# Retention attention with a routed expert layer, on one core: the tail's products ahead of the evictions in each half unit

## The chip, the core and the metric

The kernel runs on one core of a Trainium2 chip. The engines work side by side, each through its own row of instructions in a fixed order: TensorE (PE, and PEld for its weight loads) multiplies matrices into PSUM, VectorE (DVE) and ScalarE (ACT) read PSUM and work elementwise, GpSimd (POOL) does elementwise work and issues transfers, SyncE (SP) issues transfers. An instruction starts when the one before it on its engine lets it and the semaphores that it waits for have their values. The metric is the time of one execution on the device, in microseconds; less is better. TensorE's granted clock stands in the profile as a share of 2.4 GHz; 0.50 is 1.2 GHz.

## The reference

Two layers. The first is attention without a softmax: the scores of each head are weighted by a power of a per-head factor and by causality. The second sends each of 4608 tokens to one of 8 experts, 576 each.

```python
scores = scale * np.matmul(q, k.transpose(0, 1, 3, 2))        # q, k, v: 8 x 8 heads x 576 x 64
gamma = 1.0 - 2.0 ** (-5.0 - np.arange(H, dtype=np.float32))
rel = pos[:, None] - pos[None, :]
Dmat = np.where(rel >= 0, gamma[:, None, None] ** rel[None, :, :], 0.0)
attn = np.matmul(scores * Dmat[None, :, :, :], v)

logits = x @ w_gate                                           # x: 4608 x 512, the attention's output
# tokens are given to experts in order of their logits, 576 to each
for e in range(E):
    h = np.maximum(x[mask] @ w1[e], 0.0)
    out[mask] = h @ w2[e]
```

## The kernel before

**Three stages.** The attention runs until about 158 us; then the tokens are routed (logits, counting, a search for the threshold of each expert); from about 190 us on the experts' two matrix products fill TensorE to the end. All that the change touches is in the attention.

**A unit.** The attention has 16 units, `u` = 0 to 15; one unit is two heads of each of two batch entries. The 576 tokens of a head are four chunks of 128 and a tail of 64. The weighting by powers is split: the values are scaled by one power as they come in (`vscale`, on GpSimd), and the results are multiplied by another as they leave PSUM (`evict`). What remains is a causal mask inside a chunk and, across chunks, a running sum of k times v, the state.

**A half unit.** Each unit has two passes through the loop at line 769, `hf` = 0 for chunks 0 and 1, `hf` = 1 for chunks 2 and 3 and the tail. In a pass stand, in this order:

- `A` (L564): the scores of the next half unit, 8 products into the tile `pA`, and VectorE's mask (L566) on them into `am`. There is one buffer of `pA`, so the next scores wait until the mask has read the last ones. With `hf` = 0 also `A2`, the tail's scores (L575) and their mask (L577).
- `across` (L599): the products of queries with the state, into `pX`, the tile that collects the results; one buffer, two PSUM banks of 512 columns, of which 256 are for chunks 2 and 3 and 64 for the tail.
- `ST` (L587): one chunk's products of keys and values added to the state in `pS`, and ScalarE's copy of it (L589).
- `within` (L608): masked scores times values, into `pX`.
- `evict` (L628): VectorE multiplies the results by their powers on the way from `pX` to `xT`.
- `ST` once more, for the next chunk (with `hf` = 1 that is chunk 0 of the next unit).
- With `hf` = 1: the tail's products, `within2` (L615) and `across` for chunk 4 (L599), and the tail's `evict` (L628, 128x128).
- `fills`: the routing's work, put by hand at numbered places `g` (nine in a unit): logits (`logits`, L641 and L647; `logits2`, L654 and L656), transposes of rows (L665), the counting's tables.

In the last unit the second eviction is cut in two, chunk 2 and chunk 3.

**What sets the order.** The instructions of every engine stand in the order in which this code calls them (`tc.manual_schedule()`); no scheduler moves them. A layer beneath puts in the waits: an instruction that touches a tile waits for the earlier ones that wrote or read the same stretch of it. It takes a strided access as one stretch from its first to its last column, so the tail's columns of `pX` count as touched by the eviction of chunks 2 and 3, and the other way round.

**Loads.** `ahead` calls the loads of unit `u + 2` during unit `u`, with three buffers each; they stand on SyncE in one row with the stores of finished rows to DRAM (L670), which wait for VectorE's transposes (L665).

Of the kernel before, what the change touches and what calls it, by code (L numbers as in the profile page):

```python
# [497 lines left out]
def attention(tc, nc, P, qk, vk, cst_d, wg_d, rf, xd, Lg):  # L498
# [69 lines left out]
    def A2(u):  # L568

        k, q = LD[u, 'k'], LD[u, 'q']  # L570
        pa = P['ps'].tile([128, 2, 64], F32, name="pAt", tag="y", bufs=2)
        for h in range(2):
            for r in range(2):
                s = slice(1024 + 64*(h ^ r), 1088 + 64*(h ^ r))
                nc.tensor.matmul(pa[half(r), h], k[half(r), s], q[half(r), s], start=True, stop=True, skip_group_check=True)  # L575
        AM[u, 2] = P['w'].tile([128, 2, 64], F32, name="amt", bufs=2)
        nc.vector.tensor_tensor(AM[u, 2], pa, m2[:, None, :].to_broadcast([128, 2, 64]), op=ALU.mult)  # L577

    def ST(u, c):

        if u == 16: return
        if c == 0: PS[u] = PS2[:, 2*(u % 2):2*(u % 2)+2]
        v, n = LD[u, 'v'], LD[u, 'n']
        for b in range(2):
            for h in range(2):
                s = slice(256*c + 128*b + 64*h, 256*c + 128*b + 64*h + 64)
                nc.tensor.matmul(PS[u][half(h ^ b), b], n[:, s], v[:, s], start=(c == 0 and b == 0), stop=False, skip_group_check=True)  # L587
        st = P['w'].tile([128, 2, 64], F32, name="S", bufs=4)
        nc.scalar.activation(st, PS[u], AF.Copy)  # L589
        SI[u, c] = st  # L590

    def across(u, cs):

        q = LD[u, 'q']
        for c in cs:
            for h, b in FOUR:
                r = half(h ^ b)
                o, a = (PX[u, c//2][half(h), b, 128*(c % 2):128*(c % 2)+128], 256*c + 128*b) if c < 4 else (PX[u, 1][half(h), b, 256:320], 1024 + 64*b)
                nc.tensor.matmul(o, SI[u, c-1][r, b, :], q[r, a:a+o.shape[1]], start=c in (1, 2), stop=False, skip_group_check=True)  # L599

    def within(u, hf):

        v = LD[u, 'v']
        for j in range(4):
            c, b = divmod(j, 2)
            for h in range(2):
                a = 512*hf + 128*j + 64*h
                nc.tensor.matmul(PX[u, hf][half(h), b, 128*c:128*c+128], v[:, a:a+64], AM[u, hf][:, h ^ b, j],  # L608
                                 start=False, stop=False, skip_group_check=True)
# [8 lines left out]
    def evict(u, c0, c1):  # L618

        bp, hp = divmod(u, HP)  # L620
        if c0 == 4:
            src, dst, e = PX[u, 1][:, :, 256:320], XT[bp][:, hp, 1024:].rearrange("p (b i) -> p b i", b=2), ex[:, hp, None, 512:].to_broadcast([128, 2, 64])
        else:
            n, o = c1 - c0, 128*(c0 % 2)
            src = PX[u, c0//2][:, :, o:o+128*n].rearrange("p b (c i) -> p b c i", i=128)
            dst = XT[bp][:, hp, 256*c0:256*c1].rearrange("p (c b i) -> p b c i", b=2, i=128)
            e = ex[:, hp, None, 128*c0:128*c1].rearrange("p o (c i) -> p o c i", i=128).to_broadcast([128, 2, n, 128])
        nc.vector.tensor_tensor(dst, src, e, op=ALU.mult)  # L628
# [83 lines left out]
    for bp in range(NP):  # L712
        g0 = (bp+1)*4*NB + 2
        for k, b0 in enumerate((0, 3, 6)):
# [3 lines left out]
            c0 = bp*NB + b0  # L718
# [30 lines left out]
    def ahead(g):  # L749

        u, blk = divmod(g, NB)
        if u + 2 < 16:
            if blk == 3:
                load(u + 2, "kq")
            if blk == 5:
                load(u + 2, "v")
            if blk == 6:
                load(u + 2, "n")
        if u + 1 < 16:
            if blk == 2:  # L760
                vscale(u + 1, 0, 4)
            if blk == 5:
                vscale(u + 1, 4, 9)

    def fills(gs):
        for g in gs:
            for f, a in fill.get(g, []): f(*a)

    for u in range(16):
        for hf in range(2):  # L770
            gs = range(NB*u + 4*hf, NB*u + 4 + 5*hf)
            for g in gs:
                ahead(g)
            if hf == 0 and u % HP == 0:
                XT[u//HP] = P['xt'].tile([128, HP, 1152], F32, name="xT")
            A(u + hf, 1 - hf)
            if hf == 0:
                A2(u)
            PX[u, hf] = two.tile([128, 2, 512], F32, name="pX", tag="X", bufs=1)
            across(u, (2, 3) if hf else (1,))  # L780
            ST(u, 1 + 2*hf)
            within(u, hf)
            if u == 15 and hf:
                for c in (2, 3):
                    evict(u, c, c + 1)
            else:
                evict(u, 2*hf, 2*hf + 2)
            ST(u + hf, 2 - 2*hf)
            if hf:
                within2(u)  # L790
                across(u, (4,))
                evict(u, 4, 5)
            fills(gs)
    P['close']()
# [16 lines left out]
    c = R.first_digits(30, 36)  # L811
# [320 lines left out]
```

## Time and profile before

| | |
|---|---|
| median of 3 runs | 666.03 us (663.08 to 666.48) |
| the profiled execution: device time | 664.57 us |
| the profiled execution: span | 662.8 us |
| TensorE busy | 613.2 us, 93% of the span |
| VectorE busy | 418.0 us, 63% |
| ScalarE busy | 244.8 us, 37% |
| GpSimd busy | 179.0 us, 27% |
| chain that ended last, share by engine | TensorE 66%, VectorE 17%, DMA 8% |

The span runs from the first to the last instruction in the trace; the device time has the start and end around it. The shares are averages over the three stages, and in the experts' stage TensorE alone is full; so what the change is worth is read from the timeline before 165 us, unit by unit: a row of it gives when an engine starts a group of equal instructions, for how long, and, in brackets, how long the engine had been idle and what ended that. Matmuls overlap, so the spacing of two starts says more than their lengths.

### The profile page before, as it was taken

How to read it: one execution, taken by the hardware profiler on the slowest of the kernel's cores; microseconds unless marked ns; L12 is line 12 of the kernel's file. 1: busy time of each engine (PE TensorE's matmuls, PEld its weight loads, DVE VectorE, ACT ScalarE, POOL GpSimd, SP SyncE). 2: the span in 40 equal slices, each digit the busy share in tenths (PEclk: the TensorE clock that was granted, in tenths of full speed). 3: DMA queues.
4: the chain of work that ended last, by engine and by line, in shares of the span. 5: the costliest groups of instructions: out<-in, count | busy, mean ns of one | idle time of the engine just before them, and what ended most of it. 6: DMA issues, size and time to landing. Idle time of an engine off the chain costs nothing.

```text
span 662.8 us, 14684 instructions
## 1 busy us (share of the span) xinstructions
PE 613.2 (93%) x5756; PEld 522.0 (79%) x5756; DVE 418.0 (63%) x1504; ACT 244.8 (37%) x424; POOL 179.0 (27%) x221
## 2 busy tenths in 40 slices
PE   7889797978887998999999999999999999999995
PEld 5777676756557886987897798879879989988974
DVE  3586968778864987888897799689775302311200
ACT  1111020112235434455356146424624734653501
POOL 2331122120041107125143241323224135131111
PEclk8999897998997999999999999999999999999998
DMA  9996797973459548969589749928975896893521
GB/s 328 401 372 205 251 332 257 300 242 95 145 176 231 112 142 223 234 182 235 173 197 243 205 116 214 254 83 204 233 203 139 203 255 165 191 248 110 97 63 40
DMA packets 51702, 134.19 MB, mean 202 GB/s; under 512 B 5810, under 2 KB 19762, under 8 KB 51634
## 3 DMA queue, kind: packets, MB, share of 16 engines
q1 hardware_dynamic: 36530, 81.08, 35.8%
q0 software_dynamic: 14960, 51.91, 35.4%
q8 instruction: 45, 0.74, 0.5%
q10 hardware_dynamic: 144, 0.26, 0.1%
q14 instruction: 23, 0.19, 0.1%
HBM read 81.33 MB, written 18.87 MB: 151 GB/s over the span
## 4 chain that ended last, share of the span: by engine, by line
PE 66%; DVE 17%; DMA 8%; issue 5%; ACT 2%; POOL 2%; SPq 0%; POOLq 0%; DVEq 0%; ACTq 0%
PE ph L960 24%; PE py L999 24%; PE pA L564 4%; PE pX L608 3%; DVE xT L628 2%; DMA qin<-in_qk 2%; PE pX L599 2%; DMA raw<-in_w 2%; PE pS L587 2%; PE pt L931 2%; PE r L332 1%; DMA w1l<-raw 1%; PE pT L641 1%; DMA w2l<-raw 1%; DVE am L566 1%
## 5 line engine op out<-in xcount | busy, mean ns | idle before, releaser
L999 PE MATMUL py<-w2h,hb 128*128 128x512 f32 x576 | 188.2, 399 | 0.0
L960 PE MATMUL ph<-xh,w1h 128*128 128x320 f32 (+1 forms) x512 | 153.3, 303 | 2.4 <-ACT xh L933 1.9
L960 PE MATMUL ph<-xh,w1l 128*128 128x320 f32 (+1 forms) x512 | 150.7, 298 | 3.4 <-DMA w1l<-raw 3.4
L960 PE MATMUL ph<-xl,w1h 128*128 128x320 f32 (+1 forms) x512 | 150.6, 298 | 0.0
L999 PE MATMUL py<-w2l,hb 128*128 128x512 f32 (+1 forms) x320 | 125.4, 392 | 0.7 <-DMA w2l<-raw 0.7
L999 PEld LDWEIGHTS py<-w2h,hb 128*128 128x128 f32 x576 | 104.0, 188 | 20.6
L960 PEld LDWEIGHTS ph<-xh,w1h 128*128 128x128 f32 x512 | 97.3, 191 | 4.4 <-ACT xh L933 2.8
L960 PEld LDWEIGHTS ph<-xh,w1l 128*128 128x128 f32 x512 | 97.5, 192 | 3.6 <-DMA w1l<-raw 3.6
L960 PEld LDWEIGHTS ph<-xl,w1h 128*128 128x128 f32 x512 | 97.5, 192 | 0.5 <-DVE cs L336 0.3
L967 DVE SCALAR_TENSOR_TENSOR hb<-ph,hb 128x256 fp32r<-128x256 f32 (+1 forms) x192 | 59.0, 351 | 57.3 <-ACT hb L964 56.6
L964 ACT ACTIVATE hb<-ph 128x256 fp32r<-128x256 f32 (+1 forms) x128 | 52.3, 409 | 106.4 <-PE ph L960 106.4
L976 POOL DMA_INDIRECT out_y<-yt,idx x40 | 41.1, 1027 | 119.4 <-ACT yt L1016 76.7
L999 PEld LDWEIGHTS py<-w2l,hb 128*128 128x128 f32 (+1 forms) x320 | 56.7, 177 | 14.4 <-DMA w2l<-raw 1.8
L546 POOL TENSOR_TENSOR vin<-vin,cst 128x512 f32<-128x512 f32 (+1 forms) x32 | 37.6, 1194 | 106.3 <-DMA vin<-in_vk 88.2
L905 POOL DMA_DIRECT2D w2l<-raw x32 | 28.8, 899 | 122.8 <-ACT hb L964 117.6
L589 ACT ACTIVATE S<-pS 128x128 f32<-128x128 f32 x64 | 17.8, 278 | 119.4 <-PE pS L587 119.4
L916 POOL DMA_INDIRECT xg<-xd,idx x40 | 41.3, 1032 | 73.4 <-DMA raw<-in_w 40.1
L1016 ACT ACTIVATE yt<-py 128x512 f32<-128x512 f32 x32 | 19.2, 599 | 105.4 <-PE py L999 80.0
L566 DVE TENSOR_TENSOR am<-pA,cst 128x1024 f32<-128x1024 f32 x32 | 39.0, 1220 | 21.6 <-PE pA L564 21.6
L1019 DVE TENSOR_TENSOR yt<-yt,py 64x512 f32<-64x512 f32 x8 | 5.4, 679 | 70.3 <-ACT yt L1018 70.2
L564 PEld LDWEIGHTS pA<-qin,kin 64*128 64x128 f32 x512 | 34.3, 204 | 11.8 <-issue 2.7
L564 PE MATMUL pA<-qin,kin 64*128 64x128 f32 x512 | 40.8, 303 | 3.0 <-DMA qin<-in_qk 2.6
(177 smaller groups left out, 892.5 us busy)
## 6 DMA issues: line engine op xcount, KB each, us to landing
raw<-in_w SPq DMA_DIRECT2D x64, 512.0 KB, 5.1
w2l<-raw POOLq DMA_DIRECT2D x32, 512.0 KB, 5.7
w1l<-raw POOLq DMA_DIRECT2D x31, 512.0 KB, 7.2
kin<-in_qk SPq DMA_DIRECT2D x14, 576.0 KB, 8.1
qin<-in_qk SPq DMA_DIRECT2D x14, 576.0 KB, 7.5
vin<-in_vk SPq DMA_DIRECT2D x14, 576.0 KB, 7.4
nin<-in_vk SPq DMA_DIRECT2D x14, 512.0 KB, 8.2
xd<-xr SPq DMA_DIRECT2D x36, 192.0 KB, 3.8
```

The source lines that it names most:

```text
L546: nc.gpsimd.tensor_tensor(v, v, vs[:, u % HP, 2*a:2*b, None].to_broadcast([128, 2*(b-a), 64]), op=ALU.mult)
L564: nc.tensor.matmul(pa[:, r, j], LD[u, 'k'][half(r), s], LD[u, 'q'][half(r), s], start=True, stop=True, skip_group_check=True)
L566: nc.vector.tensor_tensor(AM[u, hf], pa, m1[:, None, None, :].to_broadcast([128, 2, 4, 128]), op=ALU.mult)
L608: nc.tensor.matmul(PX[u, hf][half(h), b, 128*c:128*c+128], v[:, a:a+64], AM[u, hf][:, h ^ b, j], start=False, stop=False, skip_group_check ...
L905: nc.gpsimd.dma_start(lo, raw, accum_op=ALU.add)
L916: nc.gpsimd.indirect_dma_start(out=xg[:n, j, :], out_offset=None, in_=xd[:, :], in_offset=bass.IndirectOffsetOnAxis(ap=found[e][:n, j:j+1] ...
L960: T.matmul(ps, w, x, start=(k == 0), stop=(k == 11))
L964: A.activation(hb[:, f, c], ps, AF.Relu)
L967: V.scalar_tensor_tensor(hb[:, f, to+a:to+b], ps[:, a:b], 0.0, hb[:, f, 256*s+a:256*s+b].bitcast(F32), op0=ALU.max, op1=ALU.subtract)
L976: st = nc.gpsimd.indirect_dma_start(out=out[:, :], out_offset=bass.IndirectOffsetOnAxis(ap=found[e][:n, t:t+1], axis=0), in_=y[:n], in_off ...
L999: T.matmul(ps[:m], a, w, start=(k == 0), stop=(k == last), skip_group_check=True)
L1016: A.activation(y, ps, AF.Copy)
```

## The change

In each half unit the big eviction moves behind the second state product and, with `hf` = 1, behind the tail's products; then come the evictions, the big one and the tail's. In the second half of the last unit one of the fills, the logits of chunks 0 to 2 of the last batch entries (`logits`, L641, four matmuls and ScalarE's copy), moves from behind the evictions to a place ahead of the values.

```diff
             across(u, (2, 3) if hf else (1,))
             ST(u, 1 + 2*hf)
+            if u == 15 and hf:
+                fills(gs[:1])
+                gs = gs[1:]
             within(u, hf)
-            if u == 15 and hf:
-                for c in (2, 3):
-                    evict(u, c, c + 1)
-            else:
-                evict(u, 2*hf, 2*hf + 2)
             ST(u + hf, 2 - 2*hf)
             if hf:
                 within2(u)
                 across(u, (4,))
+            for c0, c1 in ((2, 3), (3, 4)) if u == 15 and hf else ((2*hf, 2*hf + 2),):
+                evict(u, c0, c1)
+            if hf:
                 evict(u, 4, 5)
             fills(gs)
```

TensorE, from the values of unit 1's second half to the first products of unit 2, before (`L608` values, `L587` state, `L615` and the `L599` behind it the tail, `L564` scores, `L575` the tail's scores, `L599` products with the state; DVE, Activation, Pool and DMAHW name whom a row waits for):

```order
L608 MATMUL pX<-am,vin 64x128 x8
L587 MATMUL pS<-vin,nin 64x64 [waits DMAHW5_49,DMAHW6_49,Activation_49,Pool_49]
L587 MATMUL pS<-vin,nin 64x64 x3
L615 MATMUL pX<-amt,vin 64x64 [waits DVE_49]
L615 MATMUL pX<-amt,vin 64x64 x3
L599 MATMUL pX<-qin,S 64x64 x4
L564 MATMUL pA<-qin,kin 128x128 [waits PE_49]
L564 MATMUL pA<-qin,kin 128x128 x7
L575 MATMUL pAt<-qin,kin 64x64 x4
L599 MATMUL pX<-qin,S 64x128 [waits DVE_49,Activation_49]
```

and now:

```order
L608 MATMUL pX<-am,vin 64x128 x8
L587 MATMUL pS<-vin,nin 64x64 [waits DMAHW5_49,DMAHW6_49,Activation_49,Pool_49]
L587 MATMUL pS<-vin,nin 64x64 x3
L615 MATMUL pX<-amt,vin 64x64 x4
L599 MATMUL pX<-qin,S 64x64 x4
L564 MATMUL pA<-qin,kin 128x128 [waits DVE_49]
L564 MATMUL pA<-qin,kin 128x128 x7
L575 MATMUL pAt<-qin,kin 64x64 x4
L599 MATMUL pX<-qin,S 64x128 [waits DVE_49,PE_49,Activation_49]
```

The order of the matmuls is the same. The wait for VectorE has left the tail's products (L615) and stands at the next unit's scores (L564).

VectorE, the same place, before (`L566` mask of the next unit's scores, `L628` the big and the small eviction, `L577` mask of the tail's scores):

```order
L566 TENSOR_TENSOR am<-pA,cst 128x1024 [waits DVE_49,PE_49]
L628 TENSOR_TENSOR xT<-pX,cst 128x2x2x128 [waits PE_49]
L628 TENSOR_TENSOR xT<-pX,cst 128x128 [waits PE_49]
L566 TENSOR_TENSOR am<-pA,cst 128x1024 [waits DVE_49,PE_49]
L577 TENSOR_TENSOR amt<-pAt,cst 128x128 [waits PE_49]
```

and now:

```order
L566 TENSOR_TENSOR am<-pA,cst 128x1024 [waits DVE_49,PE_49]
L628 TENSOR_TENSOR xT<-pX,cst 128x2x2x128 [waits PE_49]
L628 TENSOR_TENSOR xT<-pX,cst 128x128
L566 TENSOR_TENSOR am<-pA,cst 128x1024 [waits DVE_49,PE_49]
L577 TENSOR_TENSOR amt<-pAt,cst 128x128 [waits PE_49]
```

The order is the same; the small eviction has no wait of its own any more, since the big one ahead of it now waits for the last of the tail's matmuls. In the first half of a unit neither the order nor the waits change.

TensorE at the end of the last unit, before (`L641` logits, `L654` their transposes):

```order
L587 MATMUL pS<-vin,nin 64x64 x4
L608 MATMUL pX<-am,vin 64x128 x8
L615 MATMUL pX<-amt,vin 64x64 [waits DVE_49]
L615 MATMUL pX<-amt,vin 64x64 x3
L599 MATMUL pX<-qin,S 64x64 [waits Activation_49]
L599 MATMUL pX<-qin,S 64x64 x3
L641 MATMUL pT<-xT,wg 32x384 x4
L654 MATMUL pT<-ident,lt 128x128 [waits Activation_49]
```

and now:

```order
L587 MATMUL pS<-vin,nin 64x64 x4
L641 MATMUL pT<-xT,wg 32x384 x4
L608 MATMUL pX<-am,vin 64x128 x8
L615 MATMUL pX<-amt,vin 64x64 x4
L599 MATMUL pX<-qin,S 64x64 [waits Activation_49]
L599 MATMUL pX<-qin,S 64x64 x3
L654 MATMUL pT<-ident,lt 128x128 [waits Activation_49]
```

The first logits (L641) have moved from behind the tail to ahead of the values; the transposes that wait for ScalarE's copy of them stay where they were.

## Rows read from the trace of the kernel before

**Rows 1.** Waits, 0 to 165 us: who for whom, total, times, longest.

```profile
PE pX L615 <- DVE xT L628: 19.9, 16, 3.9
...
DVE xT L628 <- PE pX L599: 9.6, 16, 0.8
```

**Rows 2.** Timeline, ends of units 1 and 13: start, length, engine, work, [idle before].

```profile
24.75 0.40 PE L587 MATMUL pS<-vin,nin 128*64 128x64 f32 x8
24.97 0.69 DVE L628 TENSOR_TENSOR xT<-pX,cst 128x512 f32<-128x512 f32 x1 [0.64 <-PE pX L608]
...
25.72 0.34 PE L615 MATMUL pX<-amt,vin 64*64 64x64 f32 x8 [0.56 <-DVE xT L628]
...
26.25 0.29 DVE L628 TENSOR_TENSOR xT<-pX,cst 128x128 f32<-128x128 f32 x1 [0.58 <-PE pX L599]
...
137.21 0.34 PE L615 MATMUL pX<-amt,vin 64*64 64x64 f32 x8 [0.56 <-DVE xT L628]
```

**Rows 3.** Timeline, first half of unit 2: state product and next scores.

```profile
28.96 0.40 PE L587 MATMUL pS<-vin,nin 128*64 128x64 f32 x8
...
29.29 1.16 PE L564 MATMUL pA<-qin,kin 64*128 64x128 f32 x16
```

**Rows 4.** Timeline, scores of unit 2.

```profile
21.91 1.16 PE L564 MATMUL pA<-qin,kin 64*128 64x128 f32 x16 [0.84 <-DMA qin<-in_qk]
```

**Rows 5.** Timeline, unit 3: masks on VectorE, then the scores behind the tail.

```profile
35.11 1.22 DVE L566 TENSOR_TENSOR am<-pA,cst 128x1024 f32<-128x1024 f32 x1
...
39.66 1.21 DVE L566 TENSOR_TENSOR am<-pA,cst 128x1024 f32<-128x1024 f32 x1
...
41.91 0.38 PE L564 MATMUL pA<-qin,kin 64*128 64x128 f32 x2
```

**Rows 6.** Timeline, end of unit 6: mask, tail's products, next scores.

```profile
68.58 1.22 DVE L566 TENSOR_TENSOR am<-pA,cst 128x1024 f32<-128x1024 f32 x1
...
70.45 0.34 PE L615 MATMUL pX<-amt,vin 64*64 64x64 f32 x8 [3.57 <-DVE xT L628]
...
70.84 2.02 PE L564 MATMUL pA<-qin,kin 64*128 64x128 f32 x16
```

**Rows 7.** Timeline, SyncE: when the loads of units 10 and 14 were issued.

```profile
86.47 0.70 SPq L516 DMA_DIRECT2D qin<-in_qk  x1
...
125.97 0.97 SPq L516 DMA_DIRECT2D qin<-in_qk  x1
```

**Rows 8.** DMA issues at 86.5 and 126.0 us: size, us to landing.

```profile
qin<-in_qk SPq DMA_DIRECT2D x1, 576.0 KB, 6.4
...
qin<-in_qk SPq DMA_DIRECT2D x1, 576.0 KB, 7.3
```

**Rows 9.** Timeline, scores of units 10 and 14.

```profile
93.58 1.16 PE L564 MATMUL pA<-qin,kin 64*128 64x128 f32 x16
...
133.40 1.16 PE L564 MATMUL pA<-qin,kin 64*128 64x128 f32 x16
```

**Rows 10.** Timeline, end of unit 10: mask and next scores.

```profile
107.55 1.21 DVE L566 TENSOR_TENSOR am<-pA,cst 128x1024 f32<-128x1024 f32 x1
...
110.04 0.80 PE L564 MATMUL pA<-qin,kin 64*128 64x128 f32 x4
```

**Rows 11.** Timeline, end of unit 14: mask and next scores.

```profile
147.07 1.22 DVE L566 TENSOR_TENSOR am<-pA,cst 128x1024 f32<-128x1024 f32 x1
...
149.33 2.00 PE L564 MATMUL pA<-qin,kin 64*128 64x128 f32 x16
```

**Rows 12.** Timeline, end of unit 15: tail's products and the first logits' transposes.

```profile
157.45 0.34 PE L615 MATMUL pX<-amt,vin 64*64 64x64 f32 x8 [0.86 <-DVE xT L628]
...
159.31 0.55 PE L654 MATMUL pT<-ident,lt 128*128 128x128 f32 x3 [0.61 <-ACT lt L647]
```

**Rows 13.** Busy time by stretch: each engine's us, then granted clock, DMA share, GB/s.

```profile
41.00:50.00 9.00, 7.92 (x168) 6.44 (x168) 6.33 (x9) 1.60 (x5) 3.97 (x4) 1.00 0.90 334
72.00:74.00 2.00, 2.00 (x28) 1.45 (x26) 1.93 (x4) 0.00 (x0) 1.85 (x2) 0.50 0.32 74
```

## The prediction

> **What bounds the kernel now.** I read the waits of the stretch before 165 us first, because all that the diff touches runs there. TensorE waits 19.9 us in front of the tail's products (`within2`, L615) for VectorE's eviction (L628), once in each of the 16 units; VectorE in turn waits 9.6 us, also 16 times, about 0.60 us each, for the last matmul of `across` (L599) before the small eviction [rows 1]. The two engines hand the work to and fro. The timeline of unit 1's end shows the handover: the state product starts at 24.75, the big eviction runs from 24.97 to 25.66, the tail's product starts at 25.72, and the small eviction only at 26.25, after an idle 0.58 us. Unit 13 has the same 0.56 us wait [rows 2]. So the wait is on the path wherever nothing else is later. I then looked for what is later: VectorE's other work (units 2, 3, 6, 10, 14), or the loads (units 0, 8, 12).
>
> After 165 us the program is the same on every engine; what starts earlier there ends earlier by as much, since its first links (logits, counting, search, gather) hang on the attention's last results.
>
> **The change part by part.** No instruction is added or removed, and VectorE's order is the same row for row. TensorE's order differs in four matmuls of the last unit only. What changes is the waits: the tail's products no longer wait for VectorE; the big eviction now waits for the tail's last matmul, the small one for nothing new; and the next score product (L564) now itself waits for the mask of the product before it (L566), which the removed wait had covered.
>
> *A unit in which TensorE is the later one.* In the first half of unit 2, without such a wait, the next product starts 0.33 us after the state product (28.96 to 29.29) [rows 3]. At the end of unit 1 it is 0.97 us (24.75 to 25.72) [rows 2]. The difference, 0.64 us, is what TensorE gains. The eviction pays for it: it starts after the tail's products, some 0.6 us later against TensorE, but the two evictions (0.69 and 0.29 us) then run without the idle 0.58 between them, so the small one ends about when it ended before. The next `across` product, which needs it, comes only after a score product of 1.16 us [rows 3] and the tail's scores; I cost this at nothing, and if that cover were gone it would cost up to 0.6 us in each of these units.
>
> *Unit 0.* The scores of unit 2 wait for their load until 21.91 [rows 4]. A gain before that is swallowed: 0.
>
> *Units 1, 4, 5, 9, 13.* TensorE is the later one and nothing after it holds it: 5 x 0.64 = 3.2.
>
> *Unit 2.* Its mask at 35.11 follows on VectorE without idle time, and so does the one at 39.66 (the routing's tables are set up there) [rows 5]. VectorE's pace is not changed by what TensorE gains here: 0, and 0.64 as the upper end.
>
> *Unit 3.* VectorE's mask ends at 39.66 + 1.21 = 40.87. The next score product came at 41.91, behind eviction and tail; now it needs only the mask, and can start some 0.05 after it: 41.91 - 40.92 = 0.99 [rows 5]. VectorE itself gains only its idle 0.60, the lower end; but after this unit TensorE is again the later one, so I take 0.99.
>
> *Unit 6.* The same picture (mask ends 69.80, tail at 70.45, scores at 70.84), but VectorE stays the later one afterwards [rows 6]: its 0.60 counts, not the 1.0 of TensorE.
>
> *Units 7 and 8.* Together 1.28 on TensorE, but the scores of unit 10 start at 93.58 and their load was issued at 86.47 and took 6.4, so it landed at 92.87 [rows 7 to 9]. Its issue stands on SyncE behind stores of rows that VectorE makes, and these move with VectorE, not with TensorE. A start some 0.1 after the landing leaves 0.6 of the 1.28.
>
> *Unit 10.* Mask ends at 107.55 + 1.21 = 108.76, scores at 110.04 [rows 10]: 1.23, as TensorE is the later one behind it (lower end 0.60).
>
> *Units 11 and 12.* The load of unit 14 was issued at 125.97 and took 7.3; it landed at 133.27 and the scores started at 133.40 [rows 7 to 9]. There the load already is the last to come, so 0 of 1.28 is kept.
>
> *Unit 14.* Mask ends 148.29, scores at 149.33 [rows 11]: 0.99 for TensorE, 0.60 for VectorE; both meet at the next eviction, so I take the middle, 0.8.
>
> *Unit 15.* The waits before the tail's products (0.86) and before the transposes of the logits (0.61, for ScalarE's copy) [rows 12] both go, since a gate product and its copy now lie beside the values: 1.47. But VectorE's three evictions, about 1.0 us, now stand behind the tail's products and ahead of the first reduction of the logits, which takes some 0.3 back. 1.2, with the ends 0.61 (only the copy's wait) and 1.47.
>
> The sum: 3.2 + 0.99 + 0.60 + 0.6 + 1.23 + 0.8 + 1.2 = 8.62. The profiled execution took 664.57 us (its span is 662.8): 664.57 - 8.6 = 656.0. The median of the three timed runs, 666.03, is 1.5 above it, which would give 657.4; I say **656.5**.
>
> **The clock.** After unit 6's wait of 3.57 us [rows 6] the granted clock in 72 to 74 us was 0.50, the 1.2 GHz level; after unit 3's shorter wait it stayed at 1.00 (41 to 50 us) [rows 13]. In the new order the tail's products are done before that wait and the scores start before the eviction, so TensorE's idle time in units 6, 10 and 14 shrinks by about one us each. Whether the clock still falls I can't tell from these rows. I forecast that it does. The Trainium skill ("TensorE: Matmul & The Clock Gate", section "What's actually happening") says that the throttled state is the default and that activity releases it; no row here decides at which length of wait. By that rule alone, shorter waits could spare the slow stretches: which is the first rival below. Without the sentences on the page the forecast is the same.
>
> **The rivals.**
> - *The clock stays up behind units 10 and 14.* A stretch of 2 us at 0.50, as that of 72 to 74 [rows 13], holds 1 us of work at 1.00. With one such stretch behind each of the two units that is 2 us of TensorE; VectorE's masks come next and hide, by my estimate, half of it: 1.0 more, 655.5. For it and against it stand the two rows named above. (The page's rule, too, would make this of it.)
> - *The loads come earlier with the rest.* Then what I took off comes back: 0.64 for unit 2, 0.68 for units 7 and 8, 1.28 for units 11 and 12, and with the clock's 1.0 in the best case 8.6 + 3.6 = 12.2: 653.8 from the median, 652.4 from the profiled execution. For it: the loads' buffers are freed earlier too, as the tail's products are what they wait for. Against it: the landing of unit 14's load [rows 8] hangs on VectorE's stores.
> - *The loads take nearly all of the light units.* Each unit's loads must pass in less time now. If they come last in every unit with TensorE later, the 3.2 and the 0.6 go, and 4.8 is left: 659.8. For it: units 0, 8 and 12 are that close. Against it: unit 1's and unit 13's neighbours show no wait for a load at all [rows 2, 3].
> - *The waits that stay fall so that the clock drops more often.* At the price above, 1 us for each stretch like that of 72 to 74, nine new ones in TensorE's stage eat the 8.6, and twelve give 664.57 - 8.6 + 12 = 668.0, slower than before. For it: the slow stretch in rows 13 follows a wait of TensorE, and such waits remain in units 6, 10 and 14. Against it: all of TensorE's waits that I find get shorter.
> - *The change doesn't do what it says*: the wait could come back at another instruction, at the next score product or at `across`. Then some 0 to 2 us are left, 663.5. For it: the score product does get a VectorE wait now. Against it: in light units that mask is done before the values even start, so it ends no wait.
>
> **How the numbers follow.** My case 0.50; the clock stays up 0.14; the loads come earlier 0.13; the loads take more 0.13; the clock drops more often 0.04; no effect 0.06. A measurement of this kernel tells about 0.5% from no change, 3.3 us. The first four are faster by more than that (0.90; 659.8 is 0.7% below its 664.57), no effect and a part of the case of more drops are within it (0.07), the rest of that case is slower (0.03). My own case runs from 654 to 659, by the ends of units 3, 10, 14 and 15 (together -1.8 and +0.5) and the 1.5 between profiled and timed runs. For eight in ten the range takes in the first three rivals with some of that spread: 652.5 to 660.5.
>
> **What would show it.** Of the 19.9 us before L615 nearly nothing is left, and the 9.6 us before the small eviction is gone; instead L564 waits for the mask (L566) in units 3, 6, 10 and 14 alone, two to three us each. The attention's last reductions (L656) begin 7 to 9 us earlier, and the rest of the span has its old length. Unit 14's scores still wait for their load. I am wrong if L599 or L564 waits for L628 in most units (the evictions then stand on the path), or if the time after the attention changes its length by more than a microsecond or two.

## The result, and the profile after

The changed kernel took **657.31 us** in the median of 13 runs (654.16 to 661.99), the kernel before beside it 663.95 (13 runs): ratio 0.9895, 95% interval 0.9870 to 0.9921, so 5.2 to 8.6 us less, in the middle 7.0. The profiled execution took 656.27 us with a span of 654.5, against 664.57 and 662.8: 8.3 us less. One thing sets the two profiled executions apart from the timed ones: over the whole execution their granted clock was 0.978 before and 0.987 after (the highest of the changed kernel's 13), while the means of the timed runs are 0.981 (all the runs of before beside the experiments) and 0.982 (the 13).

The waits of the stretch to 160 us in the changed kernel (engine, what waits <- whom for: total us, times, longest):

```profile
DVE xT L628 <- PE pX L599: 14.3, 13, 1.4
...
PE pA L564 <- DVE am L566: 9.7, 6, 2.3
...
PE pA L564 <- DMA qin<-in_qk: 2.8, 3, 1.9
...
PE pX L599 <- DVE xT L628: 1.7, 1, 1.7
```

Against [rows 1], the 19.9 us in front of the tail's products are gone; L615 waits for VectorE nowhere. The 9.6 us before the small eviction are gone as well, but VectorE's wait for `across` has grown to 14.3: it now stands before the big eviction, 1.1 us each time. That eviction's wait for the values (L608) has shrunk in return, from 12.1 to 5.8, so VectorE waits in front of its evictions nearly as long as before, 20.1 us for 21.7. Of VectorE's work, TensorE now waits for the mask and once (unit 15's first `across`) for an eviction; the rest of its waits are for loads. The timeline of unit 1's end shows the new order, and answers to [rows 2]:

```profile
23.81 0.40 PE L587 MATMUL pS<-vin,nin 128*64 128x64 f32 x8
...
24.14 0.34 PE L615 MATMUL pX<-amt,vin 64*64 64x64 f32 x8
...
24.53 1.16 PE L564 MATMUL pA<-qin,kin 64*128 64x128 f32 x16
24.67 0.89 DVE L628 TENSOR_TENSOR xT<-pX,cst 128x512 f32<-128x512 f32 x2 [1.28 <-PE pX L599]
...
27.12 0.45 PE L599 MATMUL pX<-qin,S 64*64 64x128 f32 x8 [1.05 <-issue]
```

From the state product to the tail 0.33 us (it was 0.97), as the prediction had it from [rows 3]; the two evictions run on end. The last row is new: TensorE idles 1.05 us there and waits for nothing that the trace shows (`issue`). The scores that still wait, from the timeline of the changed kernel: the two in unit 7's passes, the first of them right behind unit 6 as in [rows 6], and those of units 10 and 14 as in [rows 9]:

```profile
66.81 1.29 PE L564 MATMUL pA<-qin,kin 64*128 64x128 f32 x16 [2.30 <-DVE am L566]
...
73.04 1.16 PE L564 MATMUL pA<-qin,kin 64*128 64x128 f32 x16 [1.12 <-DVE am L566]
...
89.84 1.16 PE L564 MATMUL pA<-qin,kin 64*128 64x128 f32 x16 [0.61 <-DMA qin<-in_qk]
...
127.33 1.16 PE L564 MATMUL pA<-qin,kin 64*128 64x128 f32 x16 [0.80 <-DVE Lg L656]
```

The last one's load was issued at 120.34 and took 6.9 us, so it landed at 127.24: that is the wait's end, and not the small reduction named there. Unit 11 repeats the pair of 66.81 and 73.04 (2.23 at 104.06, right behind unit 10, and 1.12 at 110.33); behind unit 14 it is 2.09 at 141.07. The clock in these places (columns as in [rows 13]):

```profile
68.00:70.00 2.00, 2.00 (x31) 1.63 (x31) 1.90 (x6) 0.10 (x1) 1.18 (x2) 0.50 0.29 84
...
106.00:108.00 2.00, 2.00 (x27) 1.85 (x24) 1.93 (x3) 0.28 (x1) 1.94 (x2) 0.50 0.46 109
141.00:147.00 6.00, 4.25 (x91) 3.62 (x93) 5.86 (x18) 0.56 (x2) 0.00 (x0) 1.00 0.36 88
```

In this execution it falls to 1.2 GHz behind units 6 and 10 for 3.4 us each, and stays at 2.4 GHz behind unit 14. In the profiled execution of the kernel before it fell for 3.4 us behind unit 6, 6.8 behind unit 10 and 3.4 behind unit 14.

Where the time went, by how much earlier an instruction starts than before: the scores that the first pass of units 3, 6, 10 and 14 makes (+0.94, +2.76, +4.38, +6.70 us), the last unit's first L656 (+9.39), and the end (+8.27).

| stretch | forecast, us | measured, us |
|---|---|---|
| units 0 to 2 | 0.64 | 0.94 |
| units 3 to 5 | 2.27 | 1.82 |
| units 6 to 9 | 1.84 | 1.62 |
| units 10 to 13 | 1.87 | 2.32 |
| units 14, 15 | 2.00 | 2.69 |
| after the attention | 0 | -1.12 |
| sum | 8.62 | 8.27 |

The loss behind the attention is one transfer, the first expert's weights; from the chain of waits of before and of after (start, us):

```profile
196.80 8.32 DMA w1l<-raw
```

```profile
187.50 10.94 DMA w1l<-raw
```

It is issued 9.3 us earlier and lands 6.7 us earlier; a part of the difference comes back later.

### The profile page after: what moved, and what is told of

The parts are those of the page before. It is cut to its first block, busy times and chain, and to the rows that moved or that the text cites. A ratio compares the mean times of both kernels' runs of the same rounds, so it can differ in the third digit from the quotient of the medians.

```text
span 654.5 us, 14685 instructions
## 1 busy us (share of the span) xinstructions
PE 610.3 (93%) x5756; PEld 519.8 (79%) x5756; DVE 415.7 (64%) x1504; ACT 244.8 (37%) x424; POOL 179.2 (27%) x221
## 4 chain that ended last, share of the span: by engine, by line
PE 68%; DVE 15%; DMA 8%; issue 5%; ACT 1%; POOL 1%; SPq 1%; POOLq 0%; DVEq 0%; ACTq 0%
PE ph L961 26%; PE py L1000 24%; PE pA L564 4%; DMA qin<-in_qk 3%; PE pX L608 3%; PE pS L587 2%; PE pX L599 2%; DMA w1l<-raw 2%; PE pt L932 2%; PE r L332 2%; DMA w2l<-raw 1%; PE pT L641 1%; DMA cst<-in_cst 1%; DVE xr L665 1%; DVE am L566 1%
## 5 line engine op out<-in xcount | busy, mean ns | idle before, releaser
L1000 PEld LDWEIGHTS py<-w2l,hb 128*128 128x128 f32 (+1 forms) x320 | 56.7, 177 | 13.8 <-DMA w2l<-raw 1.2
L564 PE MATMUL pA<-qin,kin 64*128 64x128 f32 x512 | 38.5, 289 | 13.4 <-DVE am L566 9.7
L566 DVE TENSOR_TENSOR am<-pA,cst 128x1024 f32<-128x1024 f32 x32 | 39.0, 1220 | 18.5 <-PE pA L564 18.3
L564 PEld LDWEIGHTS pA<-qin,kin 64*128 64x128 f32 x512 | 32.2, 191 | 22.8 <-DVE am L566 11.8
```

The lines of the kernel that those rows point to most:

```text
L564: nc.tensor.matmul(pa[:, r, j], LD[u, 'k'][half(r), s], LD[u, 'q'][half(r), s], start=True, stop=True, skip_group_check=True)
L566: nc.vector.tensor_tensor(AM[u, hf], pa, m1[:, None, None, :].to_broadcast([128, 2, 4, 128]), op=ALU.mult)
L1000: T.matmul(ps[:m], a, w, start=(k == 0), stop=(k == last), skip_group_check=True)
```

## The experiments

The first four split the change by units. A line `new = u in (...)` chooses the units that have the new order; the others keep the old one. Times are medians beside runs of the kernel before on the same chip (663.44 us, 35 runs).

**The units where VectorE is late.**

```diff
+            new = u in (3, 6, 10, 14)
             within(u, hf)
+            if not new: evict(u, ...)      # the big eviction, where it was
             ST(u + hf, 2 - 2*hf)
             if hf: within2(u); across(u, (4,))
+            if new: evict(u, ...)          # behind the tail
```

> New order in units 3, 6, 10 and 14 alone. By the sum of the prediction they bring 0.99 + 0.60 + 1.23 + 0.8 = 3.6 us before the routing, and up to 4.4 us if TensorE's clock stays at 1.00 behind unit 14, as it did with the whole change: time 3.6 to 4.4 us below the kernel before. Rival: each unit gives the same share of the change's gain, then these four give 4 x 0.5 = 2 us.

Measured: 660.34 us, ratio 0.9965 (0.9932 to 0.9998), 2.3 us less (0.1 to 4.5). That the four gain together is just outside the noise; the theory's 3.6 and the rival's 2 both lie in the interval, and the time doesn't tell them apart. The trace tells little more, as its execution took 667.46 us, 7 above the median. By the shift of the next unit's first scores, unit 3 gives 1.38 there, unit 6 1.09, unit 10 2.05 and unit 14 1.50; unit 7 gives 2.26 back, 0.91 of it in a wait of 2.75 us for the next mask and the rest with the clock low from 74.55.

**The ten light units**, `new = u in (1, 2, 4, 5, 7, 8, 9, 11, 12, 13)`.

> New order in the ten units 1, 2, 4, 5, 7, 8, 9, 11, 12 and 13 alone. By the sum of the prediction 5 x 0.64 + 0.6 = 3.8 us (units 2, 11 and 12 nothing). Rival: no load and no mask swallows anything, then 10 x 0.64 = 6.4 us. Second rival: TensorE, no longer paused in each unit, waits for its instructions instead (a gap that no engine ends, 1.05 us in unit 2 with the whole change), then 2 to 3 us.

Measured: 660.58 us, ratio 0.9946 (0.9911 to 0.9981), 3.6 us less (1.3 to 5.9), so the rival's 6.4 is out. Each light unit is 0.63 us shorter in the trace (for example the scores of units 4 to 6: 2.03, 2.67, 3.30 earlier). But two loads take most of it back, the scores of units 10 and 14 in this kernel's timeline:

```profile
91.43 1.16 PE L564 MATMUL pA<-qin,kin 64*128 64x128 f32 x16 [1.45 <-DMA qin<-in_qk]
...
130.41 1.58 PE L564 MATMUL pA<-qin,kin 64*128 64x128 f32 x16 [2.21 <-DMA qin<-in_qk]
```

The loads stand behind stores that hang on VectorE, and VectorE gained nothing in units 6 and 10 here. Unit 14's load was issued 3.6 us earlier than before and took 7.9 us in place of 7.3, while TensorE was 5.1 us earlier; behind the wait the clock is low for 3.4 us and takes 0.9 more. No gap without a releaser, the second rival, stands in this trace. So the 0.64 per light unit is shown, and so is that a load swallows it where TensorE alone gets faster.

**The units costed at nothing**, `new = u in (0, 2, 11, 12)`.

> New order in units 0, 2, 11 and 12 alone, the four in which the prediction counts nothing: the time stays within 0.5 us of before. Rival: nothing is swallowed, 4 x 0.64 = 2.6 us less. In the trace, the scores of unit 2 and of unit 14 start when their load lands, whatever TensorE gained before.

Measured: 662.53 us, ratio 0.9998 (0.9965 to 1.0030). In the trace units 11 and 12 give 0.64 and 0.52, and the scores of unit 14 give 0.88 back, waiting 0.98 for their load. The forecast's zero holds, and the rival's 2.6 lies outside the interval (2.3 less to 2.0 more).

**Unit 15 alone, with the gate product**, `new = u in (15,)`.

> New order and the gate product ahead of the values in unit 15 alone. By the prediction 1.2 us (0.61 to 1.47) between the last unit's start and the first reduction of its logits. Rival: the three evictions behind the tail's products hold the reductions and nothing is won, 0 us.

Measured: 662.11 us, ratio 0.9997 (0.9966 to 1.0028). The 1.2 us is within the noise of the time, so the trace has to say. The stretch from the scores that open unit 15 to the first L656 behind it is 17.55 us here with 6.8 us at the low clock; the run before it (units 0, 2, 11 and 12), with the old unit 15 and the same 6.8 us, has 18.91: 1.36 us at equal clock, by one trace of each.

**The gate product alone**, with the old order everywhere.

```diff
+            if u == 15 and hf:
+                fills(gs[:1])
+                gs = gs[1:]
             within(u, hf)
             ... (evictions, state and tail as before)
```

> The kernel before, with the order of every half unit as it was, and alone the gate product put ahead of the values in the last unit. It tells which part gives what the last unit gave. Theory (the gate's copy on ScalarE is made beside the values, so its 0.61 us wait before the logits' transposes goes): 0.3 to 0.61 us less than before. Rival 1 (the tail's wait for the eviction is on the path as well, and the gate product only fills a part of it; the gain needs the order of evictions): 0. Rival 2 (the gate product ahead of the values fills the tail's 0.86 us wait too): 1.2 us less. The slices at the last unit in the trace tell these apart; the whole time can hardly.

Measured: 663.31 us beside 662.64 before, ratio 1.0014 (0.9986 to 1.0042); the time tells nothing, as foreseen. The same stretch is 16.67 us against 17.85 before, both with 3.4 us at the low clock: 1.18 us. The end of unit 15 in this kernel's timeline:

```profile
157.40 0.34 PE L615 MATMUL pX<-amt,vin 64*64 64x64 f32 x8 [0.86 <-DVE xT L628]
...
157.79 0.55 PE L654 MATMUL pT<-ident,lt 128*128 128x128 f32 x3
```

The tail still waits its 0.86 us, yet the transposes behind it follow without the 0.61 of [rows 12], and the four gate products now lie ahead of that wait. So rival 2 held, by one trace of each: nearly all of unit 15's gain is the gate product's, and the order of the evictions adds about 0.2 there.

**Loads ahead of the stores.** The other way to what is left: the waits of units 10 and 14 for their loads.

```diff
-        if j == 2: (4 stores of the rows, nc.sync.dma_start(xd...))
+        if j == 2: done.append((bp, blk, TR[0]))
...
+                if blk % 3 == 2:
+                    at(gr + 5, store)      # the same 4 stores, five places later
```

> The changed kernel, with the stores of the rows (L670) issued five places later in the walk, so that SyncE issues the next unit's loads ahead of them. Theory (the loads of units 10 and 14 are late because their issue stands behind stores that wait for VectorE): in the changed kernel the scores of unit 10 wait 0.61 us for their load and those of unit 14 0.80 us; both waits go, up to 1.4 us less, about 656 against 657.3. Rival (the transfers' own rate sets the landing: the same bytes in less time): the loads land no earlier, 657.3 as in the changed kernel, or later if the stores now lie beside them in another unit (up to 1.4 us more).

Measured: 651.27 us, ratio 0.9837 (0.9806 to 0.9868), 10.8 us less than before. SyncE's row around unit 14's load, first in the changed kernel, then here:

```profile
116.50 3.02 SPq L670 DMA_DIRECT2D xd<-xr  x4
...
120.34 0.88 SPq L516 DMA_DIRECT2D qin<-in_qk  x1
```

```profile
112.17 0.33 SPq L516 DMA_DIRECT2D qin<-in_qk  x1
115.16 2.64 SPq L677 DMA_DIRECT2D xd<-xr  x4
```

The load passes the stores and is issued 8.2 us earlier; the scores of units 10 (90.01) and 14 (125.59) wait for nothing. That is the 1.4 us of the theory, but the trace's lead over the changed kernel is 4.5 us at the end. Another 1.45 stands between the two scores of unit 11, 3.09 us won there against 1.64 in the changed kernel: two of VectorE's instructions ahead of the mask between them are 1.45 us shorter, for a reason that comes out below. And the clock does not fall behind unit 10. It is higher in the timed runs too, 0.987 for 0.982: some 7 us less at the low level. At the 1.1 us for 3.4 that is worked out further down, up to 2.3 of the 3.9 us beyond the change could be the clock's, an estimate.

**VectorE's routing work spread.**

```diff
-                    at(g1+5+i//2, next, it, None)
+                    at(g1+5+(i if bp < 2 else i//2), next, it, None)
...
-            at(g0+22+i//3, next, it, None)
+            at(g0+(26 if bp < 2 else 22)+i//3, next, it, None)
...
-            at(g0+24+2*n, R.first_table, ...)
+            at(g0+(30 if bp < 2 else 24)+2*n, R.first_table, ...)
```

> The changed kernel, with VectorE's work of the routing's first pass spread: the counting's steps one to a place and the digits and tables some places later for the two first pairs of blocks, so that the masks of units 6 and 10 have less VectorE work ahead of them. Theory (what is left of the wait in units 3, 6, 10 is VectorE's own work ahead of the mask, 2.3 us each in units 6 and 10, while VectorE has slack in the units between): the waits shrink to under 1 us each and what follows is 2 to 3 us earlier, about 655. Rival (VectorE's total work bounds these stretches, or the work moved comes last in the next unit or at the routing): the waits move to other units, 657.3 within 0.7.

Measured: **650.19 us**, ratio 0.9819 (0.9785 to 0.9853), 12.0 us less than before, and 5.0 beyond the change (by the two ratios; by their intervals about 2.2 to 7.8). The waits for the mask do not go but are cut into pieces: 1.19, 0.64 and 0.81 behind unit 6 and in the passes after it, 1.36, 0.64 and 0.69 behind unit 10. The total of each group (2.6 and 2.7) is 0.7 to 0.8 less than the changed kernel's 3.4, and the clock stays up (columns as in [rows 13]):

```profile
64.00:74.00 10.00, 7.63 (x159) 6.68 (x161) 9.86 (x22) 1.11 (x4) 2.26 (x2) 1.00 0.91 280
100.00:110.00 10.00, 8.04 (x167) 7.09 (x169) 9.86 (x24) 1.11 (x4) 2.26 (x2) 1.00 0.84 246
```

VectorE is still full there (9.86 of 10 us). So the direction of the theory came out, with about twice the 2 to 3 us that it forecast, and less through the waits than it said. The timed runs' clock is 0.987, as with the later stores. How the 5.0 us divide between waits, clock and the loads, for which the scores of units 10 and 14 don't wait here, these runs don't say.

**The clock held up by products without a use.**

```diff
+            if u in (7, 11, 15) and hf == 0:
+                P['warm'](8)
             A(u + hf, 1 - hf)
```

> The changed kernel, with eight matmuls without a use ahead of the score products of units 7, 11 and 15, within the waits of 2.1 to 2.3 us there for VectorE's mask. Theory (the granted clock falls to 0.50 behind units 6 and 10 because TensorE idles there): it stays at 1.00 at 67 to 71 and 105 to 109 us, and the stretch behind unit 10 is up to 1 us shorter; behind unit 6 VectorE is later and nothing is gained: about 656.5. Rival 1 (the clock does not follow these waits): the stretches at 0.50 stay, 657.3. Rival 2 (the matmuls end after the mask): later by what they take beyond the wait, some 0.5 us in each of three places, about 658.5.

Measured: 655.24 us beside 662.64, ratio 0.9893 (0.9849 to 0.9937): the changed kernel's ratio. The products lie in the wait, and the clock stays at 1.00 (66 to 72 and 104 to 110 us):

```profile
64.73 1.90 PE L1082 MATMUL warm<-full 128*128 128x512 bf16 x8
67.01 1.16 PE L564 MATMUL pA<-qin,kin 64*128 64x128 f32 x16 [0.38 <-DVE am L566]
...
73.17 1.05 PE L564 MATMUL pA<-qin,kin 64*128 64x128 f32 x14 [2.60 <-DVE am L566]
```

So products in the wait hold the clock up, but a faster TensorE only waits longer for the next mask: 2.60 us in place of 1.12 in unit 7, and 2.41 in unit 11. Behind these two waits, longer than the 2.30 and 2.23 of the changed kernel, the clock stays at 1.00 as well; that TensorE's idleness alone brings the low clock is not shown. The timed runs' clock rose from 0.982 to 0.987, some 6 us less at the low level, at the same ratio: holding it up behind units 6 and 10 is worth nothing that these runs can measure.

**Both edits at once, and both in the old order.** The runs of the kernel before beside the next three have a median of 663.07 us (11 runs).

> The changed kernel with the later stores of the rows and with VectorE's routing work spread, both at once (each alone: 651.3 and 650.2). Theory (two separate limits, the loads of units 10 and 14 and VectorE in units 3, 6 and 10): the gains add, 657.3 - 6.0 - 7.1 = 644.2. Rival (both take away the same thing, since the row stores and the loads behind them hang on VectorE, and a lighter VectorE brings the loads early by itself): about 650, no better than the spread alone.

> The same two edits, later stores and spread VectorE work, in the kernel before, with its own order of values, evictions, state and tail. It tells what the new order is worth where nothing else holds the units up. Theory (TensorE then bounds nearly every unit, and each gains its 0.64 us): slower than the run with the new order by 14 x 0.64 + 1.2 = 10.2 us, near 658. Rival (the order is worth the same 7 us with either): slower than the run with the new order by 7. Rival 2 (the old order's wait is filled by the work that the spread moves): by under 4.

Measured: with the new order 651.10 us, ratio 0.9825 (0.9796 to 0.9854); with the old one 654.59, ratio 0.9889 (0.9861 to 0.9916). The gains do not add: the rival held, no better than the spread alone. And the order, worth 7.0 us in the kernel that the prediction is about, is worth 4.2 here (0.65%, by the two intervals about 1.6 to 6.9): the theory's 10.2 is out, and between the two rivals, 7 and under 4, the runs don't decide. The clock is likely a part of why; two stretches of the run with the new order, and one of the run with the old:

```profile
72.00:74.00 2.00, 2.00 (x32) 1.45 (x30) 1.93 (x6) 0.00 (x0) 0.00 (x0) 0.50 0.86 291
...
108.00:110.00 2.00, 2.00 (x30) 1.45 (x30) 1.97 (x5) 0.00 (x0) 0.00 (x0) 0.50 1.05 369
```

```profile
100.00:116.00 16.00, 14.05 (x293) 11.63 (x291) 14.66 (x35) 2.22 (x8) 4.84 (x4) 1.00 0.96 342
```

In its profiled execution the new order has 10.2 us at the low clock before 113 us, and loses 1.7 and 2.5 us of its lead there; the old order has none from 12 us to the end of the attention. The timed runs agree: their mean clock is 0.985 with the new order and 0.989 with the old, about 5 us more at the low level. That the clock alone makes the difference is not shown.

**Unit 14 spread as well**: counting steps one to a place for the third pair too, its last three row transposes two to five places later.

> The run with both edits, and VectorE's work before unit 15 spread too: the counting's steps of the third pair one to a place, and the last three row transposes of that pair two to five places later, into unit 15. With the spread alone, the second scores of unit 14 wait 2.09 us for VectorE's mask and the across products of unit 15 wait 1.69 us for its eviction, while VectorE idles 3.0 us behind that. Theory: those waits fall to under 2 us together, and the routing begins about 2 us earlier: 2 us less than the run with both edits. Rival (what is moved comes last in unit 15 and at the logits): 0, or up to 2 us more.

Measured: 652.02 us, ratio 0.9827 (0.9797 to 0.9858), no better than both edits. In the profiled execution the attention ends 3.0 us earlier (first L656 at 144.43 against 147.42), though `across` waits 2.47 us for VectorE; behind it the counting waits 1.91, the clock is low for 6.8 us from 152.5, and 1.8 us are left at the end. The timed runs show none of it: the rival held.

**Without GpSimd's scaling.** The same VectorE instructions had different lengths in these traces. In the changed kernel (GpSimd's scaling first):

```profile
99.74 2.58 POOL L546 TENSOR_TENSOR vin<-vin,cst 128x512 f32<-128x512 f32 x2 [6.18 <-DMA vin<-in_vk]
100.28 0.92 DVE L219 TENSOR_TENSOR G<-rc_f,m 128x384 bf16<-128x384 f32 x1
...
101.12 1.28 DVE L209 TENSOR_TENSOR oh<-t,mx 128x72 bf16<-128x72 bf16 x1
102.33 0.55 DVE L219 TENSOR_TENSOR G<-rc_f,m 128x384 bf16<-128x384 f32 x1
102.80 1.21 DVE L566 TENSOR_TENSOR am<-pA,cst 128x1024 f32<-128x1024 f32 x1
```

L219 takes 0.92 beside GpSimd and 0.55 behind it. The test leaves the scaling out for five units:

```diff
-        if u + 1 < 16:
+        if u + 1 < 16 and u + 1 not in (7, 8, 11, 12, 15):
             if blk == 2:
                 vscale(u + 1, 0, 4)
```

> The changed kernel, with GpSimd's scaling of the values (L546) left out for units 7, 8, 11, 12 and 15, so that its output isn't the reference's; the rest of the program is the same. In the changed kernel ten of VectorE's routing instructions before 150 us take 7.2 us longer in all than the same instructions elsewhere (a mask of 0.16 takes 1.02, an equality of 0.22 takes 1.28), each of them while GpSimd scales values of one of these five units; in the kernel before it is 4.3 us. Theory (the two engines hinder each other, and this takes a part of the change's gain): without the scaling these instructions have their short times, the masks of units 6, 10 and 14 come 3.0, 3.2 and 1.0 us earlier, of which what TensorE's wait of 2.1 to 2.3 us there and 1.1 us in the next half leaves room for is gained: 4 to 7 us, 650 to 653. Rival 1 (these instructions are long for another reason, their data or their place): they stay long, 657.3. Rival 2 (they get short, but the loads or the clock take it back): short instructions, less than 2 us, 655.5 to 657.3.

Measured: 653.05 us beside 664.95, ratio 0.9812 (0.9777 to 0.9847): 12.5 us less than before, where the changed kernel has 7.0. The same instructions here:

```profile
97.67 0.52 DVE L219 TENSOR_TENSOR G<-rc_f,m 128x384 bf16<-128x384 f32 x1
98.11 0.22 DVE L209 TENSOR_TENSOR oh<-t,mx 128x72 bf16<-128x72 bf16 x1
98.25 0.55 DVE L219 TENSOR_TENSOR G<-rc_f,m 128x384 bf16<-128x384 f32 x1
98.72 1.22 DVE L566 TENSOR_TENSOR am<-pA,cst 128x1024 f32<-128x1024 f32 x1
```

None is long any more, and the waits for unit 10's mask are 1.09 and 0.90 us in place of 2.23 and 1.12. So both rivals are out, and the time came out as the theory has it, with 5.5 us (by the intervals about 2.6 to 8.4) against the 4 to 7 expected. A part of it is the clock again, which does not fall behind units 6 and 10 here and is 0.990 in the timed runs for 0.982: at the same 1.1 us for 3.4, up to 3.5 of the 5.5. What the run does not tell is whether the change made VectorE's instructions any longer; the old order without the scaling was not run. The expectation's 4.3 us for the kernel before is too low. Against their lengths in this run, nine of its routing instructions take 6.7 us longer between 45 and 150 us, and ten of the changed kernel's take 7.3. Behind unit 14, first in the kernel before, then in the changed kernel, then without the scaling:

```profile
143.16 0.88 DVE L199 TENSOR_TENSOR t<-Lg,m 128x72 bf16<-128x72 f32 x1
144.08 1.15 DVE L201 TENSOR_TENSOR t<-t,decb 128x72 bf16<-128x72 bf16 x1
```

```profile
136.73 0.92 DVE L201 TENSOR_TENSOR t<-t,decb 128x72 bf16<-128x72 bf16 x1
138.46 0.81 DVE L219 TENSOR_TENSOR G<-rc_f,m 128x384 bf16<-128x384 f32 x1
```

```profile
131.33 0.23 DVE L199 TENSOR_TENSOR t<-Lg,m 128x72 bf16<-128x72 f32 x1
131.60 0.20 DVE L201 TENSOR_TENSOR t<-t,decb 128x72 bf16<-128x72 bf16 x1
```

## Why the prediction was right, and where not

**The main step held.** One light unit is worth 0.64 us by the prediction and 0.63 to 0.64 in the trace; the eviction that pays for it is hidden, and no L599 or L564 of a light unit waits for it. The zeros held too: units 11 and 12 alone give nothing that the time shows, since unit 14's load comes last. In the whole change they keep about half a microsecond, as that load was issued 5.6 us earlier.

**The size, and the luck in it.** The sum was 8.62, and the timed runs gave 7.0 (5.2 to 8.6): it was some 1.6 too large, at the interval's edge; which term that is, the timed runs can't say. The forecast of 656.5 came within a microsecond of 657.31 because the time that it was taken from was too large as well: 656.5 + 8.62 is 665.1, between the profiled 664.57 and the 666.03 of three runs, where 13 runs give 663.95. From that the sum makes 655.3. That these two cancelled was luck. A part of the 8.27 in the trace is luck too: the clock's, as shown below.

**The units where VectorE is late** (0.99, 0.60, 1.23, 0.8). The waits for the mask stood at 2.1 to 2.3 us behind units 6, 10 and 14, as forecast, with 1.12 more in the second passes of units 7 and 11. What the working lacked is that VectorE's pace there is not fixed: its short routing instructions stretch beside GpSimd's scaling, in the old order and in the new, by amounts that differ from trace to trace. Measured against the run without the scaling and taken off, they leave a rest that can be compared. The stretches run from the scores of the unit's first pass to those of unit 7's second pass, unit 11's second and unit 15's first; in each row TensorE spent the same time at the low clock:

| stretch | order | length, us | stretched by, us | rest, us | gain of the rest, us | forecast, us |
|---|---|---|---|---|---|---|
| unit 6, low clock 3.4 us | old (before) | 16.28 | 2.77 | 13.51 | | |
| | new (changed kernel) | 15.82 | 3.02 | 12.80 | 0.71 | 0.60 |
| unit 10, low clock 3.4 us | old (four runs) | 15.81 to 16.37 | 2.28 to 2.85 | 13.52 to 13.77 | | |
| | new (changed kernel) | 16.14 | 3.26 | 12.88 | 0.64 to 0.89 | 1.23, lower end 0.60 |
| unit 14, no low clock | old (before) | 10.95 | 1.59 | 9.36 | | |
| | new (changed kernel) | 9.39 | 1.02 | 8.37 | 0.99 | 0.8 |

The four runs are those of the ten light units, of units 0, 2, 11 and 12, of unit 15 and of the gate product. The gains are estimates, as they take VectorE to set the length throughout. By them units 6 and 14 came out near what the working had. Unit 10 is nearer the lower end of its forecast: these four runs pass its stretch in the changed kernel's time without the new order, while the trace that the 1.23 was read from takes 17.4 us, with the low clock for 6.8. For unit 3 the traces don't tell: its 0.55 in the changed kernel lies within the 0 to 0.6 that runs with the old order there show against the same trace.

**The clock.** "I forecast that it does" fall behind units 6, 10 and 14: in the profiled execution it did behind 6 and 10, for 3.4 us less behind 10 than before, and not behind 14. That looks like half of the first rival. Its price was 1 us for a stretch. One stretch of 3.4 us measures 1.13: from the scores that open unit 15 to the first L656 it is 17.85 us before and 16.72 in the run with the ten light units, with the same work there and no low clock. Behind unit 10, where before has 3.4 us more of it than the four runs, the rest is 15.0 us against their 13.5 to 13.8. At equal clock the changed kernel's trace would thus have given about 1 us for units 10 to 13 in place of the forecast 1.87, and 1.56 for units 14 and 15 in place of 2.00, an estimate. The timed runs don't show this gain: by their mean clocks (0.981 and 0.982) both kernels spend about the same time at the low level, some 25 and 24 us of an execution. So the timed 7.0 us stand nearly without the clock, and the forecast that the low clock stays held on average. The clock is a likely part of why the profiled pair differs by 8.3.

**Unit 15** was right in size, 1.2 for 1.18 to 1.36, by the way that was not chosen: the gate product ahead of the values gives it, whatever the order of the evictions.

**Units 0 to 2**: a wait of 0.84 for the load [rows 4] became 1.91 in the changed kernel, as forecast, but the load itself landed 0.94 us earlier; then the 1.05 us at 27.12 took that back, by one trace of each. Neither was in the working.

**The time after the attention** lost 1.12 us, at the edge of "more than a microsecond or two". The first expert's weights took 10.94 us and not 8.32. In the twelve other runs TensorE's wait for them is between 2.6 and 4.7 us, against 3.4 before and 6.0 in the changed kernel's profiled execution, so it looks like spread between executions rather than a cost of the order; one trace of each can't settle it. The 1.3 us between the profiled gain (8.3) and the timed one (7.0) are within the timed interval.

**What the list of signs said.** Right: L615's wait gone, unit 14's load still waited for, the attention's end 7 to 9 us earlier (9.4). Half right: the small eviction's 9.6 us are gone, but VectorE waits for `across` longer than before, 14.3 us, at the big eviction, which the list doesn't have. Wrong: the waits for the mask stand behind units 6, 10 and 14 and once more in units 7 and 11, not behind unit 3.

## What to carry to other kernels

Take out a wait on the engine that is late, and then read unit by unit what comes last: here a light unit gave its whole 0.64 us only until a load that another engine's stores hold back, or a VectorE with its own work, was in front of it. As large gains lay in those two, 3.9 and 5.0 us beyond the change (by the ratios), part of them perhaps the clock's, and they overlap, so measure them together before adding them. Compare the length of the same instruction between two traces before taking an engine's pace as given. And read a term from more than one trace where the clock moves, and look at the granted clock of the timed runs: one profiled pair showed 8.3 us where 13 runs gave 7.0.

## What the runs showed of the hardware

- **GpSimd slows VectorE's short instructions.** A 128x72 bf16 equality takes 0.22 us alone and 1.28 beside a GpSimd product of two SBUF inputs; a 128x9 integer product 0.17 and 1.18. The masks and evictions, which read PSUM (L566, L628), and the transposes (L665) keep their length beside it. The Trainium skill ("GPSIMD Engine Reference", section "Specifications") says that the two engines share their SBUF interfaces, with contention for VectorE instructions with two SBUF inputs or in a two-port mode; the traces agree in which instructions are hit.
- **The low clock follows some waits and not others.** In the changed kernel it fell 0.9 and 1.2 us behind the ends of waits of 2.30 and 2.23 us, and not behind one of 2.09; without waits that long in units 6 and 10 (spread work, or no scaling) it did not fall there. With products without a use in the first wait it did not fall behind the next one, though that was longer, 2.60 and 2.41 us. With both edits it fell behind pairs of shorter ones (0.75 or 1.33 us, and 0.90 within 2 us). So the length of a wait alone does not decide; what does was not found.
- **A denser TensorE idles 1.05 us without a visible cause** at 27.12 us; five of the seven kernels with the whole new order have it, 0.83 to 1.05, and the kernel before nowhere. In these five a transfer of 16 KiB on the instruction queue starts at 24.6 to 25.1 us, 2.4 to 2.6 before TensorE goes on; in the two without the idle time (spread work, no scaling) it starts at 22.0 and 23.1. With the old order in unit 1 it starts as late as 25.7 without such a gap. That TensorE waits for its own instructions there was not tested.
